# Layer-norm output transposed by DMA crossbar instead of TensorE, in a two-layer attention and MLP kernel

## Chip, cores and metric

The kernel runs on one core of one Trainium2 chip. The metric is the device time of one execution in microseconds (us); the kernel before has a median of 1329.79 us over three runs (1329.6 to 1330.23). Engines are named as in the profile: PE is TensorE, PEld its weight loads, DVE is VectorE, ACT is ScalarE, POOL is GpSimd, SP is SyncE, which here issues nearly all DMAs (its queue is written SPq).

## What is computed

Two layers over 2048 tokens of width 1024. Each layer is a layer norm, an attention over a dilated window (32 heads of 32, 8 positions two apart), a residual, a second layer norm, an MLP with a squared ReLU (3584 wide) and a second residual. The reference, cut:

```python
def _layernorm(x, axis=-1, eps=1e-5):
    m = jnp.mean(x, axis=axis, keepdims=True)
    v = jnp.var(x, axis=axis, keepdims=True)
    return (x - m) / jnp.sqrt(v + eps)
...
    x = x + _A_ref(_layernorm(x, axis=-1), A_wqkv, A_wo)
    x = x + _B_ref(_layernorm(x, axis=-1), B_w1, B_b1, B_w2, B_b2)
    x = x + _A_ref(_layernorm(x, axis=-1), A_wqkv, A_wo)
    x = x + _B_ref(_layernorm(x, axis=-1), B_w1, B_b1, B_w2, B_b2)
```

`_A_ref` is the projection to q, k and v, the window attention and the output projection; `_B_ref` is `w1`, squared ReLU, `w2`. All matrix operands are bf16.

## The kernel before

**Units.** The tokens are cut into four blocks of 512 (`BLK`), and each block in each layer is one unit `u`, so there are eight units, 0 to 3 in layer 0 and 4 to 7 in layer 1. A block has four tiles `tl` of 128 tokens. A unit goes through six stages, each a generator:

- **SA** (`gen_SA`): loads four x tiles (`xt`), normalises each and writes it transposed into `xnT`, a buffer of 128 partitions x 8 x 512, where TensorE needs the 1024 features on the partitions.
- **SQa**, **SQb** (`gen_SQ`): the projections; 64 matmuls each for k and q (SQa) and 64 for v (SQb), line 268, eight to one PSUM tile `pq`; ACT copies each out (line 270) into kT, qT or vT.
- **S2** (`gen_S2`): the window attention, nearly all on DVE (lines 316 to 414), with small matmuls (`lg`, line 362; in unit 0 line 349) and 16 TensorE transposes of its own for each half block (`ptp`, line 398).
- **SW** (`gen_SW`): the output projection, 64 matmuls (line 457), two groups of eight for each tile; DVE adds the residual into `xm` (line 459); then the second layer norm of that tile, into a second `xnT`.
- **SF** (`gen_SF`): the MLP in two halves; 28 groups of eight matmuls `ph` (line 485), each of which reads `xnT` of all four tiles, ACT's ReLU and square (lines 489, 490), and the second product (line 506) with the residual added by DVE (lines 512 to 521). Results go to `xs` in HBM (layer 0, line 522) or to the output (line 517).

**Order.** `build` lists the main stages: SQa(0), SQb(0), then for each u SQa(u+1), SW(u), SQb(u+1), SF(u). SA and S2 are side tasks, advanced in steps between those of the main stages, by a launch position and a deadline: SA(u) is launched 30 steps before SQa(u) and paced to be done after 0.75 of them. So SA's work lies within the MLP of another unit, while between SW(u), which ends in layer norms, and SF(u), which needs them, lies only SQb(u+1), and for the last unit nothing. The order of instructions on each engine is fixed when the program is built, from this order and from priorities (`high_priority`); each engine runs its own list in order and waits by semaphores.

**The layer norm** (`ln_transpose`, lines 160 to 198) works on one tile. In most units ACT does all: a sum (line 181), a sum of squares (line 185), small steps (lines 183, 187 to 189), and the scaled copy into `xn` (line 190). In SA(0) and SW(7) (`dve_stats`) DVE takes the statistics (line 172) and ACT only scales. `xn` has two buffers (`xp`, bufs=2, line 65), and lines 181 and 185 use it as scratch, so a tile's layer norm can start only when the tile two before it has been read. Then eight TensorE transposes against an identity (line 193) go into one PSUM tile `pt`, and one copy takes it to `xnT` (line 198 on DVE; line 196 on ACT in SA(1), SA(2) and SW(0), by `evac_act`). `pt` shares two PSUM buffers with `ptp`. `xnT` has two buffers (line 217), used in turn by SA and SW. There are 64 calls of `ln_transpose`: eight units, two norms, four tiles.

**Weights** come in tiles of up to 1 MB (`wt`, five buffers, lines 143 to 158). `get_w` issues loads up to three tiles ahead (`PF` = 3) of the one it hands out, so such a load waits until the tile five before it has been used. All loads and stores of x, xs, the weights and the output are issued by SP, in one queue.

Of the kernel before, what the change touches and what calls it, by code (L numbers as in the profile page):

```python
# [6 lines left out]
BF = mybir.dt.bfloat16  # L7
# [19 lines left out]
class _Kernel:  # L27
# [132 lines left out]
    def ln_transpose(self, xt, xnT, tl, dve_stats=False, evac_act=False):  # L160
        nc = self.nc
        small = self.small
        D = self.D
        xn = self.xp.tile([128, D], BF, name="xn", tag="xn")
        rstd = small.tile([128, 1], F32, name="rstd")
        nmr = small.tile([128, 1], F32, name="nmr")
        if dve_stats:
            nsg = D // 512
            stats = small.tile([128, nsg, nc.vector.BN_STATS_DIM], F32, name="stats")
            xr = xt.rearrange("p (n f) -> p n f", f=512)  # L170
            for sg in range(nsg):
                nc.vector.bn_stats(out=stats[:, sg, :], in_=xr[:, sg, :])
            mv = small.tile([128, nc.vector.BN_AGGR_DIM], F32, name="mv")
            nc.vector.bn_aggr(out=mv[:], in_=stats[:])
            lnv = small.tile([128, 1], F32, name="lnv")
            nc.scalar.activation(out=lnv[:], in_=mv[:, 1:2], func=ACTF.Ln, bias=self.eps[:], scale=1.0)
            nc.scalar.activation(out=rstd[:], in_=lnv[:], func=ACTF.Exp, scale=-0.5)
            nc.vector.scalar_tensor_tensor(out=nmr[:], in0=mv[:, 0:1], scalar=-1.0, in1=rstd[:], op0=ALU.mult, op1=ALU.mult)
        else:
            s1 = small.tile([128, 1], F32, name="s1")  # L180
            nc.scalar.activation(out=xn[:], in_=xt, func=ACTF.Identity, accum_out=s1[:])  # L181
            nmean = small.tile([128, 1], F32, name="nmean")
            nc.scalar.activation(out=nmean[:], in_=s1[:], func=ACTF.Identity, scale=-1.0 / D)
            s2 = small.tile([128, 1], F32, name="s2")
            nc.scalar.activation(out=xn[:], in_=xt, func=ACTF.Square, bias=nmean[:], scale=1.0, accum_out=s2[:])  # L185
            lnv = small.tile([128, 1], F32, name="lnv")
            nc.scalar.activation(out=lnv[:], in_=s2[:], func=ACTF.Ln, bias=self.eps[:], scale=1.0 / D)
            nc.scalar.activation(out=rstd[:], in_=lnv[:], func=ACTF.Exp, scale=-0.5)
            nc.scalar.activation(out=nmr[:], in_=nmean[:], func=ACTF.Identity, scale=rstd[:])
        nc.scalar.activation(out=xn[:], in_=xt, func=ACTF.Identity, bias=nmr[:], scale=rstd[:])  # L190
        pt = self.ps_t.tile([128, self.KD, 128], BF, name="pt", tag="pt")
        for kd in range(self.KD):
            nc.tensor.transpose(pt[:, kd, :], xn[:, kd * 128:(kd + 1) * 128], self.ident[:])  # L193
        with self.tc.high_priority():
            if evac_act:
                nc.scalar.copy(xnT[:, :, tl * 128:(tl + 1) * 128], pt[:])
            else:
                nc.vector.tensor_copy(xnT[:, :, tl * 128:(tl + 1) * 128], pt[:])  # L198

    def load_x_tile(self, layer, t, tag):  # L200
        nc = self.nc
# [458 lines left out]
```

## Time and profile before

| | |
|---|---|
| time, three runs | 1329.79 us median, 1329.6 to 1330.23 |
| profiled execution | span 1328.2 us from its first to its last instruction; its time outside the span is not recorded, and the median of the runs is 1.6 us longer |
| granted TensorE clock, mean | 0.996 |
| busy | PE 1284.9 us, PEld 679.9, DVE 830.1, ACT 681.1 |
| DMA | 223.69 MB, 168 GB/s on average |
| TensorE transposes of the layer norm (line 193) | 512, in 64 groups of eight |
| copies of the transposed tiles | 52 on DVE (685 ns each), 12 on ACT (1010 ns median) |

The units 1 to 5 repeat each other to within a few hundredths of a microsecond, 161 us apart: what is read in the stretch from 399 to 560 us holds for them. A stretch of 161 us has the last norms of one unit (SW) near its start and SA of the unit after the next near its end. The rows used below show, in order: the start in us, the duration, the engine, the line, the operation, output<-input, shape, how many instructions were merged, and in brackets the idle time of the engine before it with what ended it.

### The profile page before, as it was taken

The numbers are of one execution on the slowest core, as the hardware profiler recorded it, in microseconds if no ns is written. First come the engines' busy times: TensorE is split into PE (matmuls) and PEld (weight loads), VectorE is DVE, ScalarE is ACT, GpSimd is POOL, SyncE is SP. The second block draws the span as 40 slices with busy tenths as digits, with TensorE's granted clock in tenths as the row PEclk, the third lists the DMA queues.
The fourth block names the chain that finished last, engine by engine and source line by source line (L and its number), as shares of the span: only waits on it lengthen the run. The fifth ranks groups of instructions, "written<-read, shape, count | busy, mean of one in ns | idle before, by whom it ended". The sixth has DMA issues, their size and how long they took to land.

```text
span 1328.2 us, 17261 instructions
## 1 busy us (share of the span) xinstructions
PE 1284.9 (97%) x6972; PEld 679.9 (51%) x7104; DVE 830.1 (63%) x1170; ACT 681.1 (51%) x1229; POOL 2.9 (0%) x9
## 2 busy tenths in 40 slices
PE   6999999999999999999999999999999999997998
PEld 3665444654446544455445554455544555443443
DVE  4599993394934949268582777719676197926011
ACT  4647826287342964239561494615836166142622
POOL 0000000000000000000000000000000000000000
PEclk9999999999999999999999999999999999999999
DMA  8434544546355554656356464456634564346441
GB/s 214 160 127 158 175 142 156 194 160 204 123 196 186 180 174 143 205 184 208 121 178 230 161 220 152 135 188 208 204 127 163 195 214 138 123 150 224 127 135 56
DMA packets 180847, 223.69 MB, mean 168 GB/s; under 512 B 8608, under 2 KB 143776, under 8 KB 180768
## 3 DMA queue, kind: packets, MB, share of 16 engines
q1 hardware_dynamic: 177168, 222.58, 50.9%
q0 software_dynamic: 3600, 0.01, 0.4%
q8 instruction: 55, 0.90, 0.3%
q14 instruction: 24, 0.20, 0.0%
HBM read 209.98 MB, written 12.58 MB: 168 GB/s over the span
## 4 chain that ended last, share of the span: by engine, by line
PE 73%; DVE 14%; ACT 11%; issue 1%; DMA 0%; SPq 0%; ACTq 0%
PE ph L485 28%; PE pq L268 12%; DVE P L316 5%; DVE P L335 4%; ACT xn L190 3%; ACT xn L181 3%; ACT xn L185 2%; PE pt L193 1%; DVE pr L411 1%; PE py L457 1%; PE ptp L398 1%; DVE xm L459 1%; ACT vT L270 1%; PE lg L362 1%; DVE pr L412 1%
## 5 line engine op out<-in xcount | busy, mean ns | idle before, releaser
L485 PE MATMUL ph<-xnT,wt 128*128 128x512 bf16 x1751 | 393.1, 380 | 3.0 <-DVE xnT L198 0.8
L268 PE MATMUL pq<-xnT,wt 128*128 128x512 bf16 x1500 | 340.7, 381 | 3.0 <-DVE xnT L198 0.8
L506 PEld LDWEIGHTS <-r2t 128*128 128x128 bf16 x1792 | 174.6, 98 | 207.0 <-ACT r2t L490 0.4
L485 PEld LDWEIGHTS <-wt 128*128 128x128 bf16 x1792 | 174.2, 98 | 206.6 <-issue 2.9
L268 PEld LDWEIGHTS <-wt 128*128 128x128 bf16 x1536 | 216.7, 144 | 107.3 <-issue 3.3
L489 ACT ACTIVATE r<-ph,b1T 128x512 bf16<-128x512 f32 x224 | 153.0, 683 | 98.3 <-PE ph L485 96.9
L411 DVE TENSOR_TENSOR pr<-pb,vT 128x2048 bf16<-128x2048 bf16 x128 | 154.5, 1221 | 44.2 <-ACT pb L399 44.2
L316 DVE TENSOR_TENSOR P<-qT,kT 128x2048 bf16<-128x2048 bf16 x128 | 153.5, 1224 | 36.8 <-ACT qT L270 36.7
L490 ACT ACTIVATE r2t<-r 128x512 bf16<-128x512 bf16 x224 | 140.7, 629 | 5.5
L270 ACT CAST kT<-pq 128x512 bf16<-128x512 f32 x64 | 37.6, 587 | 189.1 <-PE pq L268 189.1
L457 PE MATMUL py<-wt,oT 128*128 128x512 bf16 x496 | 114.0, 383 | 0.8
L335 DVE TENSOR_TENSOR P<-P 128x2048 bf16<-128x2048 bf16 x84 | 102.2, 1218 | 0.4
L412 DVE TENSOR_TENSOR pr<-pr 128x1024 bf16<-128x1024 bf16 x128 | 85.6, 682 | 0.0
L399 ACT COPY pb<-ptp 128x1024 bf16<-128x1024 bf16 x32 | 31.6, 1013 | 104.1 <-PE ptp L398 103.9
L457 PEld LDWEIGHTS <-oT 128*128 128x128 bf16 x512 | 50.1, 99 | 59.0 <-issue 2.0
L270 ACT CAST qT<-pq 128x512 bf16<-128x512 f32 x64 | 37.5, 586 | 65.3 <-PE pq L268 65.3
L193 PE MATMUL pt<-ident,xn 128*128 128x128 bf16 x512 | 41.5, 227 | 29.5 <-ACT xn L190 28.7
L193 PEld LDWEIGHTS <-xn 128*128 128x128 bf16 x512 | 32.4, 101 | 51.4 <-ACT xn L190 45.5
L279 DVE COPY khalo<-kT 128x56 bf16<-128x56 bf16 x8 | 1.4, 179 | 85.1 <-ACT kT L270 85.1
L198 DVE COPY xnT<-pt 128x1024 bf16<-128x1024 bf16 x52 | 35.6, 685 | 29.6 <-PE pt L193 29.6
L181 ACT ACTIVATE xn<-xt 128x1024 bf16<-128x1024 f32 (+1 forms) x28 | 29.5, 1053 | 44.5 <-PE pt L193 44.5
L413 DVE TENSOR_TENSOR pr<-pr 128x512 bf16<-128x512 bf16 x128 | 51.5, 416 | 0.0
(468 smaller groups left out, 1109.2 us busy)
## 6 DMA issues: line engine op xcount, KB each, us to landing
wt<-in_B_w_dram SPq DMA_DIRECT2D x88, 1024.0 KB, 6.0
wt<-in_A_wqkv_dram SPq DMA_DIRECT2D x48, 1024.0 KB, 6.1
wt<-in_B_w_dram SPq DMA_DIRECT2D x32, 768.0 KB, 4.6
wt<-in_A_wo_dram SPq DMA_DIRECT2D x16, 1024.0 KB, 6.1
xt<-xs_106 SPq DMA_DIRECT2D x32, 512.0 KB, 4.1
xt<-in_A_x_dram SPq DMA_DIRECT2D x32, 256.0 KB, 3.8
xs_106<-xof SPq DMA_DIRECT2D x32, 256.0 KB, 2.9
out_dram<-xo SPq DMA_DIRECT2D x32, 128.0 KB, 2.0
```

Source lines behind the costliest of these rows:

```text
L193: nc.tensor.transpose(pt[:, kd, :], xn[:, kd * 128:(kd + 1) * 128], self.ident[:])
L268: nc.tensor.matmul(pq[:], fetch(nm)[kd // 4][:, kd % 4, c0:D:8], xnT[:, kd, :], start=(kd == 0), stop=(kd == KD - 1))
L270: nc.scalar.copy(dst[:, c0, off:off + BLK], pq[:])
L316: pi = nc.vector.tensor_tensor(P[:], qT[:, c, None, hb * HB:(hb + 1) * HB].to_broadcast([128, W, HB]), _win_ap(kT[:, c, :], HALO + hb * HB ...
L335: nc.vector.tensor_tensor(other[:], other[:], cur[:], ALU.add)
L411: nc.vector.tensor_tensor(pr[:], pb[:], vwin, ALU.mult)
L412: nc.vector.tensor_tensor(pr[:, 0:4, :], pr[:, 0:4, :], pr[:, 4:8, :], ALU.add)
L457: nc.tensor.matmul(py[:], oT[:, c, tl * 128:(tl + 1) * 128], wos[db][:, c, :], start=(c == 0), stop=(c == NCH - 1))
L485: nc.tensor.matmul(ph[:], wt[:, kd, cc * 128:(cc + 1) * 128], xnT[:, kd, :], start=(kd == 0), stop=(kd == KD - 1))
L489: nc.scalar.activation(out=r[:], in_=ph[:], func=ACTF.Relu, bias=self.b1T[:, f_idx:f_idx + 1], scale=1.0)
L490: nc.scalar.activation(out=r2t[:], in_=r[:], func=ACTF.Square)
L506: nc.tensor.matmul(py[:], r2[kf][:, tl * 128:(tl + 1) * 128], w2s[gi][:, j, :], start=(kf == 0), stop=(kf == KFH - 1))
```

## The change

The transposes by TensorE and the copy out of PSUM are replaced by one DMA for each tile, issued by SP, that reads `xn` (128 tokens x 1024) in SBUF and writes it transposed into the 128 columns of `xnT` that belong to the tile (128 partitions x 8 x 128). With it go the PSUM tile `pt` and the choice of engine for the copy. Everything else stays, the two buffers of `xn` included, which are now read by the DMA.

```diff
         nc.scalar.activation(out=xn[:], in_=xt, func=ACTF.Identity, bias=nmr[:], scale=rstd[:])
-        pt = self.ps_t.tile([128, self.KD, 128], BF, name="pt", tag="pt")
-        for kd in range(self.KD):
-            nc.tensor.transpose(pt[:, kd, :], xn[:, kd * 128:(kd + 1) * 128], self.ident[:])
-        with self.tc.high_priority():
-            if evac_act:
-                nc.scalar.copy(xnT[:, :, tl * 128:(tl + 1) * 128], pt[:])
-            else:
-                nc.vector.tensor_copy(xnT[:, :, tl * 128:(tl + 1) * 128], pt[:])
+        nc.sync.dma_start_transpose(xnT[:, :, tl * 128:(tl + 1) * 128], xn[:])
```

## Prediction

> **What bounds the kernel now.** The page comes first: the busy times, the transposes' group, the DMA queues and issues.
>
> ```profile
> PE 1284.9 (97%) x6972; PEld 679.9 (51%) x7104; DVE 830.1 (63%) x1170; ACT 681.1 (51%) x1229; POOL 2.9 (0%) x9
> ...
> q1 hardware_dynamic: 177168, 222.58, 50.9%
> q0 software_dynamic: 3600, 0.01, 0.4%
> ...
> L193 PE MATMUL pt<-ident,xn 128*128 128x128 bf16 x512 | 41.5, 227 | 29.5 <-ACT xn L190 28.7
> ...
> xt<-in_A_x_dram SPq DMA_DIRECT2D x32, 256.0 KB, 3.8
> xs_106<-xof SPq DMA_DIRECT2D x32, 256.0 KB, 2.9
> ```
>
> PE is busy nearly all the span, so work taken from PE is worth its full time where PE has no other wait. Line 193's 29.5 us idle is 10.1 us of the start and short waits. The timeline of PE shows them where a unit goes from SW to SF:
>
> ```profile
> 426.89 9.66 PE L457 MATMUL py<-wt,oT 128*128 128x512 bf16 x43
> 437.45 0.62 PE L193 MATMUL pt<-ident,xn 128*128 128x128 bf16 x8 [0.90 <-ACT xn L190]
> 437.91 4.48 PE L457 MATMUL py<-wt,oT 128*128 128x512 bf16 x19
> 442.23 0.59 PE L268 MATMUL pq<-xnT,wt 128*128 128x512 bf16 x2
> 443.07 0.62 PE L193 MATMUL pt<-ident,xn 128*128 128x128 bf16 x8 [0.25 <-ACT xn L190]
> 443.53 5.78 PE L268 MATMUL pq<-xnT,wt 128*128 128x512 bf16 x25
> 449.50 0.62 PE L193 MATMUL pt<-ident,xn 128*128 128x128 bf16 x8 [0.19 <-ACT xn L190]
> ...
> 453.05 0.62 PE L193 MATMUL pt<-ident,xn 128*128 128x128 bf16 x8
> ...
> 459.32 1.03 PE L485 MATMUL ph<-xnT,wt 128*128 128x512 bf16 x4
> ```
>
> The next instruction starts 0.45 us after a group of eight transposes does. The last tile is transposed at 453.05, and ph starts at 459.32: 6 us of v matmuls (SQb) cover the copy. ACT is why the tiles come late; its timeline shows tile 0's norm, without a gap, and the later tiles:
>
> ```profile
> 432.58 1.06 ACT L181 ACTIVATE xn<-xm 128x1024 bf16<-128x1024 f32 x1 [4.90 <-DVE xm L459]
> ...
> 436.16 1.24 ACT L190 ACTIVATE xn<-xm,nmr,rstd 128x1024 bf16<-128x1024 f32 x1
> 437.31 1.04 ACT L181 ACTIVATE xn<-xm 128x1024 bf16<-128x1024 f32 x1
> ...
> 440.75 1.04 ACT L181 ACTIVATE xn<-xm 128x1024 bf16<-128x1024 f32 x1
> ...
> 444.29 1.04 ACT L181 ACTIVATE xn<-xm 128x1024 bf16<-128x1024 f32 x1
> ```
>
> A norm takes 4.8 us of ACT alone. Tile 2 starts (440.75) once tile 0's xn has been read (437.9), tile 3 (444.29) after tile 1's (443.5): two xn buffers.
>
> **Removed.** 64 groups x 0.45 us = 28.8 us of PE, at most. The waits in this stretch add 0.90 + 0.25 + 0.19 = 1.3 us a unit. The weight loads of the transposes lie under matmuls: nothing. 52 x 0.685 = 36 us of DVE and 12 x 1.0 us of ACT go too; neither bounds PE in the middle, so I count them only where named.
>
> **Added: 64 DMAs of 256 KB.** None is in the trace, so I bound L, the time from the end of xn to an xnT that PE may read. Below: the 256 KB store of xs, 2.9 us. The 256 KB load of xt takes 3.8. A packet of q0 (4 B) costs 0.004 x 16 x 1328.2 us / 3600 = 24 ns of an engine, one of q1 (1256 B) 61 ns: 24 ns + 0.03 ns a byte. A store of 2 KB rows is 8 packets an engine, 0.7 us, so its fixed part is 2.2 us. In rows of 128 features (256 B) the transpose is 64 packets of 31 ns, 2.0 us: L = 4.2. If each 32-byte piece (16 tokens of a feature) costs a packet, it is 512 x 25 ns = 12.8 us: L = 15, the upper end. I take 4.2, nearest the two rows of equal size. At 2.0 us each, 64 transposes add 128 us to DMA engines busy for half of 1328 us: hidden.
>
> The trace has eight 128x128 transposes in 0.45 us. The Trainium skill, page "VectorE: DVE Perf Modes", section "The three transpose paths", lists 390 ns for one on TensorE and 1309 ns on the DMA crossbar. No run here has that second figure; taken eight times it would be an estimate of 10.5 us, and by it the sum would end near 1415, slower.
>
> **The stretch again.** Without groups and waits PE reaches ph at 459.32 - 1.8 - 1.3 = 456.2. On ACT tile 0 ends at 437.4 and lands at 441.6; tile 1 ends at 442.1 and lands at 446.3, or at 449 if it queues behind the two weight loads that SP issues from 440.70 (6 us each). Tile 2 runs from 442.1, tile 3 from 446.3 to 449, with v copies of 0.57 us between them: xn of tile 3 ends between 453.6 and 455, say 454.2, and lands at 458.4. So ph gains 0.9 us, and PE idles 2.2. What is late next is this landing.
>
> Idleness has a price: in unit 0, after a wait of 2.40 us, 21 matmuls take 6.38 us where 216 ns each would make 4.5; 1.8 us lost.
>
> ```profile
> 112.27 0.62 PE L193 MATMUL pt<-ident,xn 128*128 128x128 bf16 x8 [2.40 <-ACT xn L190]
> 112.72 6.38 PE L457 MATMUL py<-wt,oT 128*128 128x512 bf16 x21
> ```
>
> I take 2.4 us as the point where it starts. The Trainium skill, page "TensorE: Matmul & The Clock Gate", section "Why this matters for your kernels", puts that point at about 3 us. No wait between 1 and 2.4 us in this trace tells more, and the row speaks against the rule; at L = 4.2 the sum is the same by both, at 4.6 it would be 1322 by the rule and 1334 by the row.
>
> **The sum, against the span of 1328.2 us:**
> - units 1 to 6: 0.9 in SW, and 4 x 0.45 = 1.8 in SA, which lies inside SF where PE is full and the landing has some 17 us (from the last transposes, 382.2, to the first pq, 399.3, in the timeline): 2.7 x 6 = 16.2 gained;
> - SA(1): 4 x 0.45 = 1.8 gained;
> - unit 0's SW: PE could be at ph at 135.16 - 1.8 - 2.7 - 1.8 = 128.9; the last xn comes at about 128.5 (130.5 less two ACT copies), lands at 132.7, and a cold restart costs 1.8: 0.7 gained;
> - last unit: xn ends at 1224.3, 1.4 earlier without two copies and a group ahead of it, lands at 1227.2, ph was at 1226.3: 0.9 lost;
> - start: xn ends at 15.0. SP issues five weight loads from 3.1 to 11.2; with x and b2b that is 6.25 MB, of which 264 GB/s bring 4.5 by 17 us. Behind all of it the last tile lands near 23.5, free of it at 19.2. Middle 21.4 against 16.93: 4.5 lost.
>
> Gain 13.3 us: span 1314.9. The runs' median is 1.6 us above the span: **1317**.
>
> SP is also passed. A transpose waits there for its xn and for its xnT buffer, with weight loads, x loads and stores behind it. A w1 tile is loaded four tiles of 6.9 us ahead and lands in 6: some 20 us of cover. If that went, each further microsecond would be PE's.
>
> **Rivals.**
> 1. **All hidden.** L = 2.9, as the store. Tile 3 lands at 456.2, when PE comes: 3.1 + 1.8 = 4.9 a unit, x 6 = 29 gained, 4 in units 0 and 1, 2 lost at the ends: 1299. For it: the bytes are the same. Against: rows cut to 256 B.
> 2. **The landing takes the wait's place, and costs more.** Each microsecond of L delays tile 3 once by itself and about once more through the xn buffers: 2 x 6 + 2 at the ends = 14 us, and past 2.4 us idle the 1.8 us restart comes on top in six units, 11 us. It decides from L of about 4.4, where PE's idle time reaches 2.4: the gain is then 13 - 3 - 11, below zero. L = 6 gives 13 - 25 - 11 = -23: 1353. L = 7.5 gives 1374. For it: ACT's chain has no slack. Against: 256 KB land in 3.8 us now.
> 3. **The crossbar bounds.** 12.8 us x 64 = 819 us of DMA on 676 now: more than the span, about 1500. Were the change to move single 2-byte elements instead of using the crossbar, 8192 x 24 ns = 197 us each, it would be ten times the span. Nothing but the small-packet row speaks for these.
> 4. **SP's order.** Tile 3's transpose queued behind the weight load that waits for the end of the v matmuls (458.65): 3 to 6 us later in each unit, with the restart: about 1350. Against: loads are listed when their buffers come free, after xn.
>
> **Chances.** Forecast (L from 3.4 to 4.4, or later without the restart: 1306 to 1328) 0.36, of which 0.03 is within 0.2% (about what a measurement tells from no change); rival 1 0.16; rival 2 0.30, of which 0.03 is within; rival 3 0.10; rival 4 0.08. Faster 0.33 + 0.16 = 0.49, same 0.06, slower 0.45. The range leaves out rival 3 and the tails of 1 and 2: 1296 to 1375. The likeliest case's own range is 1306 to 1328.
>
> **What would show it.** PE without line 193; the transposes' time to landing (4.2 right, over 4.4 wrong); PE's idle before ph in SW's last stretch (2.2 us in each unit) with DMA as its releaser; ph's first matmuls at 216 ns, not 400; ACT line 181 waiting for a DMA; the first pq near 21. What makes it wrong most easily: L, or ACT blocked by the two xn buffers ahead of the v copies.

## The result and the profile after

The changed kernel takes 1333.73 us (median of 18 runs, 1328.84 to 1337.71), the kernel before 1330.59 (18 runs beside them, 1329.52 to 1331.63). The ratio is 1.0023, with a 95% interval of 1.0015 to 1.0032: slower by 0.2%, just clear of noise, where 1.0% faster was forecast. The profiled execution took 1334.27 us, with a span of 1332.6; its mean granted TensorE clock was 0.988, against 0.996 before.

Line numbers of the changed kernel are 7 lower than before, from the transpose (now line 191) on. The page after, then its list of DMA issues and its waits (engine and line, what it waited for, total us, times, longest):

```profile
PE 1264.9 (95%) x6592; PEld 654.0 (49%) x6592; DVE 799.1 (60%) x1118; ACT 667.4 (50%) x1217; POOL 2.9 (0%) x9
...
q1 hardware_dynamic: 244752, 239.37, 58.9%
```

```profile
xnT<-xn SPq DMA_TRANSPOSE x64, 3.4
```

```profile
PE pq L261 <- DMA xnT<-xn: 23.3, 1, 23.3
PE ph L478 <- DMA xnT<-xn: 14.0, 3, 11.0
PE py L499 <- ACT r2t L483: 9.2, 8, 2.7
...
ACT xn L181 <- DMA xnT<-xn: 6.2, 13, 1.2
...
ACT xn L190 <- DMA xnT<-xn: 5.2, 2, 4.6
```

PE lost 20 us of busy time, and yet the span grew. The transposes land in 3.4 us (median, from the issue on SP), so they are not slow. Besides the forecast waits ahead of ph, three kinds of waiting are new or longer: at the start (23.3 us until the first pq, against 16.9 before), at the last unit (11.0), and, of a kind that no rival named, waits of the second MLP product (py, line 499) for ACT's square `r2t`. The starts of the stages on PE's timeline tell where the time went. Gains are positive:

| stretch | before | after | gain, us |
|---|---|---|---|
| start to SW(0), its first py | 100.85 | 109.07 | -8.2 |
| SW(0) to ph(0) | 34.31 | 32.73 | +1.6 |
| ph(0) to SQa(2) | 102.99 | 102.52 | +0.5 |
| SQa(u+1) to ph(u), units 1 to 6, each | 59.99 to 60.08 | 59.86, 57.48, 57.86, 57.38, 58.80, 58.14 | +10.8 in all |
| ph(u) to SQa(u+2), units 1 to 5, each | 101.06 to 101.07 | 101.13, 103.01, 103.11, 102.61, 101.32 | -5.8 in all |
| ph(6) to SW(7) | 99.28 | 99.28 | 0 |
| SW(7) to ph(7) | 23.19 | 24.94 | -1.7 |
| ph(7) to the end | | | -1.5 |

The sum is -4.4, the difference of the spans. So the stretch with SW's transposes gains more than forecast, and the MLP, from which four groups of TensorE transposes (1.8 us) were taken, takes 1.5 to 2.0 us longer than before in units 2, 3 and 4. PE's timeline of unit 2 after, and its last row's counterpart in unit 3:

```profile
459.64 1.93 PE L261 MATMUL pq<-xnT,wt 128*128 128x512 bf16 x8
462.79 15.70 PE L478 MATMUL ph<-xnT,wt 128*128 128x512 bf16 x72 [1.23 <-ACT xn L185]
...
488.25 1.89 PE L478 MATMUL ph<-xnT,wt 128*128 128x512 bf16 x8 [0.33 <-ACT r L482]
...
495.94 0.39 PE L499 MATMUL py<-wt,r2t 128*128 128x512 bf16 x1 [0.16 <-ACT r2t L483]
499.07 14.20 PE L499 MATMUL py<-wt,r2t 128*128 128x512 bf16 x65 [2.75 <-ACT r2t L483]
...
658.36 15.88 PE L499 MATMUL py<-wt,r2t 128*128 128x512 bf16 x65 [1.98 <-ACT r2t L483]
```

The 1.23 us ahead of ph is put down to ACT, but that instruction has nothing to do with it: SP issues the last transpose at 459.53, and ph starts 3.3 us later, a landing's time. The 2.75 us wait is the new one. In unit 3 the wait is shorter, but the same 65 matmuls take 1.7 us longer: the granted clock was 0.5, half of full speed, from 658.4 to 661.8.

Such half-clock stretches are the second thing that the change added. After the start, the clock records show 0.5 for 10.2 us of the span before and for 30.7 us after, in pieces of 3.4 us or a whole multiple of it. Half of PE's busy time in them, an estimate of what they cost, is 3.7 us before and 10.9 after. In the MLP of units 0, 1 and 5 they follow a wait ahead of ph (2.42, 3.60 and 2.54 us) and cost 1.3 to 1.7 us each; the table counts that in the row of the MLP.

ACT's timeline shows why r2t is late; first before, with the row of PE that ends its wait, then after:

```profile
489.13 0.71 ACT L489 ACTIVATE r<-ph,b1T 128x512 bf16<-128x512 f32 x1
489.87 0.63 ACT L490 ACTIVATE r2t<-r 128x512 bf16<-128x512 bf16 x1
506.56 1.93 ACT L399 COPY pb<-ptp 128x1024 bf16<-128x1024 bf16 x2 [16.06 <-PE ptp L398]
517.38 1.06 ACT L181 ACTIVATE xn<-xt 128x1024 bf16<-128x1024 f32 x1 [8.89 <-PE pt L193]
```

```profile
516.73 0.61 PE L193 MATMUL pt<-ident,xn 128*128 128x128 bf16 x8
```

```profile
468.21 1.23 ACT L190 ACTIVATE xn<-xt,nmr,rstd 128x1024 bf16<-128x1024 f32 x1
...
472.51 1.23 ACT L190 ACTIVATE xn<-xt,nmr,rstd 128x1024 bf16<-128x1024 f32 x1
...
476.07 1.06 ACT L181 ACTIVATE xn<-xt 128x1024 bf16<-128x1024 f32 x1 [1.75 <-DMA xt<-xs]
...
486.39 1.24 ACT L190 ACTIVATE xn<-xt,nmr,rstd 128x1024 bf16<-128x1024 f32 x1
...
497.25 1.25 ACT L190 ACTIVATE xn<-xt,nmr,rstd 128x1024 bf16<-128x1024 f32 x1
498.38 0.64 ACT L483 ACTIVATE r2t<-r 128x512 bf16<-128x512 bf16 x1
```

Before, ACT normalises SA's first two tiles by 461.8, ahead of the MLP's ReLUs and squares, and finishes the squares of the first half at 490.5. The third tile's norm then waits 8.9 us until TensorE has transposed the first tile and freed its xn, 57 us after that was written. After, a DMA frees xn within a few microseconds, and SA's third and fourth norm and the last step of the first two (the rows `xn<-xt`) run between the ReLUs and squares of the first half. The last square ends at 499.0, when PE's py resumes. ACT's list itself differs: the order is fixed when the program is built, and without the transposes the third and fourth norms stand earlier in it.

The start: SP's timeline, then the ACT row that waits, then PE's first row.

```profile
3.14 1.07 SPq L149 DMA_DIRECT2D wt<-in_A_wqkv_dram  x2
10.22 4.97 SPq L191 DMA_TRANSPOSE xnT<-xn  x2
15.24 0.58 SPq L149 DMA_DIRECT2D wt<-in_A_wqkv_dram  x1
18.57 2.61 SPq L191 DMA_TRANSPOSE xnT<-xn  x2
21.23 1.14 SPq L149 DMA_DIRECT2D wt<-in_A_wqkv_dram  x2
```

```profile
17.30 2.37 ACT L190 ACTIVATE xn<-xt,nmr,rstd 128x1024 bf16<-128x1024 bf16 x2 [4.58 <-DMA xnT<-xn]
```

Before, SP issued five weight loads by 11.2 us. Now it stands at the first transpose from 4.2 to 10.2 with three of the loads behind it, and tile 2's norm waits 4.6 us for tile 0's transpose to have read its xn. A late weight load costs PE another 2.6 us at 60 us, and a half-clock stretch follows.

### The profile page after: what moved, and what is told of

Read it like the earlier page. It is cut to its first block, busy times and chain, and to the rows that moved or that the text cites. A ratio compares the mean times of both kernels' runs of the same rounds, so it can differ in the third digit from the quotient of the medians.

```text
span 1332.6 us, 16456 instructions
## 1 busy us (share of the span) xinstructions
PE 1264.9 (95%) x6592; PEld 654.0 (49%) x6592; DVE 799.1 (60%) x1118; ACT 667.4 (50%) x1217; POOL 2.9 (0%) x9
## 4 chain that ended last, share of the span: by engine, by line
PE 56%; ACT 22%; DVE 12%; DMA 8%; issue 2%; SPq 0%; ACTq 0%
PE py L499 28%; PE ph L478 18%; PE pq L261 9%; DMA xnT<-xn 5%; DVE P L309 4%; ACT r L482 4%; ACT xn L181 3%; ACT xn L185 3%; ACT r2t L483 3%; ACT xn L190 3%; DVE P L328 3%; DMA xt<-in_A_x_dram 1%; DVE pr L404 1%; DMA xt<-xs 1%; ACT vT L263 1%
## 5 line engine op out<-in xcount | busy, mean ns | idle before, releaser
L478 PE MATMUL ph<-xnT,wt 128*128 128x512 bf16 x1792 | 399.4, 384 | 25.7 <-DMA xnT<-xn 14.0
L499 PE MATMUL py<-wt,r2t 128*128 128x512 bf16 x1792 | 393.6, 380 | 9.2 <-ACT r2t L483 9.2
L261 PE MATMUL pq<-xnT,wt 128*128 128x512 bf16 x1536 | 341.9, 382 | 25.9 <-DMA xnT<-xn 23.3
L509 DVE TENSOR_TENSOR xo<-py,xm 128x512 bf16<-128x512 f32 x32 | 22.1, 692 | 113.2 <-PE py L499 113.2
L505 DVE TENSOR_TENSOR xm<-py,xm 128x512 f32<-128x512 f32 x64 | 43.9, 685 | 57.5 <-PE py L499 57.5
L514 DVE TENSOR_TENSOR xof<-py,xm 128x512 f32<-128x512 f32 x32 | 22.1, 692 | 91.5 <-PE py L499 76.6
```

The costliest lines, as they stand in the source:

```text
L261: nc.tensor.matmul(pq[:], fetch(nm)[kd // 4][:, kd % 4, c0:D:8], xnT[:, kd, :], start=(kd == 0), stop=(kd == KD - 1))
L478: nc.tensor.matmul(ph[:], wt[:, kd, cc * 128:(cc + 1) * 128], xnT[:, kd, :], start=(kd == 0), stop=(kd == KD - 1))
L499: nc.tensor.matmul(py[:], r2[kf][:, tl * 128:(tl + 1) * 128], w2s[gi][:, j, :], start=(kf == 0), stop=(kf == KFH - 1))
```

## The experiments

**Theory A**: the two ends lose what the landings cost there. **Theory B**: in the middle, TensorE's transposes, at their place in PE's order, held SA's norms back by way of the two xn buffers. DMAs free SA's buffers early, so the norms are placed and run early, where ACT is busiest, and the MLP waits for ACT. **Rival C**: the middle is limited by the landing of tile 3 before ph and by the two xn buffers.

All times below are medians of 4 to 11 runs beside runs of the kernel before on the same chip (1330.2 to 1330.6). Stage times and rows are of one profiled execution each, which lies up to 5 us from its median.

**TensorE at the ends.** SA(0) and SW(7) keep the eight transposes and the copy.

```diff
+        if dma:
             nc.sync.dma_start_transpose(xnT[:, :, tl * 128:(tl + 1) * 128], xn[:])
+            return
+        pt = self.ps_t.tile([128, self.KD, 128], BF, name="pt", tag="pt")
...
-            self.ln_transpose(xt, xnT, tl, ...)
+            self.ln_transpose(xt, xnT, tl, ..., dma=(u > 0))
-            self.ln_transpose(xm[:], xnT, tl, ...)
+            self.ln_transpose(xm[:], xnT, tl, ..., dma=(u < self.n_layers * self.NB - 1))
```

> TensorE transposes are kept in SA(0) and SW(7), the two places with no other work beside them; the other 56 stay DMAs. In the trace of after, the first pq starts 6.4 us later than before, py of unit 0 8.2 later, ph of unit 0 6.6 later, and ph of the last unit loses 1.8 us more and then 1.5 us to a cold restart. Theory A (the loss is at the two ends and the middle gains a little): 1333.7 - 6.6 - 3.3 = about 1324, first pq at 17 us, ph of unit 7 less than 5 us after its py ends. Rival (the ends are swallowed later, because DVE or ACT sets the pace of unit 0): less than 4 us gained, above 1329.

Measured: 1322.26 us, ratio 0.9939 (0.9922 to 0.9957); first pq at 16.7, SW(7) to ph(7) 23.2 as before. The ends cost 11 us, a little more than A had counted. The MLP's stretches stay long (102.4, 104.0, 103.1, 102.9 and 101.2 us, half-clock stretches included); the profiled execution, 1327.2 us, was the slowest of six that spread over 9.1 us.

**SA's norms held on ACT.** All 64 stay DMAs; one ordering edge puts each SA norm behind the last square recorded before it.

```diff
-            nc.scalar.activation(out=xn[:], in_=xt, func=ACTF.Identity, accum_out=s1[:])
+            si = nc.scalar.activation(out=xn[:], in_=xt, func=ACTF.Identity, accum_out=s1[:])
+            if after is not None:
+                self.tc.add_manual_dep(si.ins, after.name, ...NoSync..., reason="hold the norm on ACT")
...
-            self.ln_transpose(xt, xnT, tl, ...)
+            self.ln_transpose(xt, xnT, tl, ..., after=self.last_r2)
...
-                        nc.scalar.activation(out=r2t[:], in_=r[:], func=ACTF.Square)
+                        self.last_r2 = nc.scalar.activation(out=r2t[:], in_=r[:], func=ACTF.Square).ins
```

> All 64 transposes stay DMAs; the first sum of each SA norm is put behind the last squared-ReLU instruction recorded before it on ACT (an order on one engine, no semaphore), so SA's norms can't run early in the MLP. Theory B (in the middle the gain is given back in SF, since without the TensorE transposes SA's norms run early, among ACT's ReLU and square of the first half, and py waits for r2t): the stretch from ph to the next SQa falls from 101.1 to 103.1 us in units 1 to 5 to about 99.3 each, 12 to 15 us in all, time 1319 to 1322, py's waits for r2t (9.2 us) near 0. Rival C (the middle is limited by the landing of tile 3 before ph): SF changes little, time within 3 us of 1333.7.

Measured: 1319.97 us, ratio 0.9913 (0.9900 to 0.9926), as B expected and far from C. The MLP stretch is 101.7, 100.2, 100.2, 100.2 and 101.9 us in units 1 to 5. Of the 12.2 us between the two spans, 7.0 are there and 2.4 from SW(0) to ph(0); the MLP alone gave less than the 12 to 15 that B had put on it. PE's waits for r2t fall from 9.2 to 4.4 us. Units 1 and 5 are longer by a half-clock stretch behind a wait ahead of ph (2.58 and 2.44 us); in all, these stretches cost 4.0 us less than in the changed kernel's profile (6.9 against 10.9, the same estimate), which is part of the 12.2 and which the hold was not made to change. PE's timeline of unit 3, second half of the MLP:

```profile
675.87 20.88 PE L483 MATMUL ph<-xnT,wt 128*128 128x512 bf16 x96
696.59 2.54 PE L504 MATMUL py<-wt,r2t 128*128 128x512 bf16 x11
699.86 18.52 PE L504 MATMUL py<-wt,r2t 128*128 128x512 bf16 x85 [0.73 <-ACT r2t L488]
718.22 1.03 PE L266 MATMUL pq<-xnT,wt 128*128 128x512 bf16 x4
```

The first half has no wait for r2t left; one of 0.73 us is new in the second half, where the norms now are. It is most of the difference between the 100.2 of a unit and the 99.3 expected.

**DMAs in SW alone** (28; `dma=False` in SA, and in SW as in the first experiment).

> DMA transposes only in SW(0) to SW(6), 28 of 64; SA and SW(7) keep TensorE. Theory B: SA's transposes at their place in TensorE's order hold SA's norms back as before, so SF keeps its 101.1 us, and the stretch from SQa to ph keeps what the DMAs gained (60.05 before, 57.4 to 58.8 in units 2 to 5 of after): 1 to 2.6 us in each of six units, time 1315 to 1325. Rival C: SW is where the landing hurts, so 1328 to 1335.

Measured: 1319.41 us, ratio 0.9919 (0.9906 to 0.9932). SQa to ph takes 57.5 to 58.3 us in units 2 to 6, and the MLP 101.06 to 101.07 in units 2 to 5: TensorE's transposes of SA hold its norms back again (the third norm of unit 3 waits 8.9 us for them, as before the change), and no wait for r2t is left. Rival C as a reason for the loss falls: SW is where the DMAs gain.

**DMAs in SA alone** (28; `dma=False` in SW, no hold).

> The mirror of the kernel with DMAs in SW alone: DMAs only in SA(1) to SA(7), not held; SA(0) and all SW keep TensorE. Theory B (SA's norms, no longer held by TensorE's order, run early and delay r2t): the stretch from ph to the next SQa is 101 to 103.5 us, no gain although 1.8 us of TensorE work left it, SQa to ph stays at 60.05 or grows: 1326 to 1335. If the crowding needs SW's DMAs as well, SF falls to 99.3 us: about 1318.

Measured: 1331.90 us, ratio 1.0006 (0.9997 to 1.0015). 12.6 us of TensorE work (28 groups of 0.45) went, for nothing. SQa to ph is 60.0 as before, the MLP 99.9 to 102.2, and PE waits 8.8 us for r2t. B holds without SW's DMAs too.

Two rows of unit 0 in this run bear on the prediction's price of idleness. They are at the place where before 21 matmuls took 6.38 us after a wait of 2.40:

```profile
110.94 0.62 PE L196 MATMUL pt<-ident,xn 128*128 128x128 bf16 x8 [2.38 <-ACT xn L190]
111.40 4.70 PE L460 MATMUL py<-wt,oT 128*128 128x512 bf16 x21
```

**Four xn buffers** in the changed kernel (`tag="xn", bufs=4`).

> The changed kernel with four xn buffers in place of two. Rival C (landing times two xn buffers limits the middle and the start): ACT waits at the xn writes (11.4 us of waits for xnT DMAs in all) vanish, ph comes about 2 us earlier in six units and the first pq 4 us earlier: about 1318. Theory B (SA's norms run early because nothing holds them): the start gains up to 4 us, but with more buffers SA's norms can run ahead still more, so SF loses as much or more than now: 1330 to 1337.

Measured: 1326.56 us, ratio 0.9969 (0.9957 to 0.9981): between the two expectations. The first pq comes at 20.4 and SW(0) at 103.2, so of the 8.2 us lost by SW(0) the two buffers made 5.9. The other 2.3 need not be the landing: with TensorE at the start, the hold and four buffers (below) the first pq comes at 16.8, and SW(0) still at 102.1, against 100.85 before. The MLP takes 100.6 to 101.6 in units 1 to 5, where B had expected as much as in the changed kernel or more, but SQa to ph is 58.4 to 58.6 in units 2 to 5. The crowd has moved: two of SA's norms now run on ACT around the last one of SW. PE's timeline of unit 3:

```profile
619.18 15.70 PE L478 MATMUL ph<-xnT,wt 128*128 128x512 bf16 x72 [2.13 <-ACT nmean L183]
```

ACT starts the last xn of SW 53.9 us after SQa (614.67 against 560.80), and the first of SA's at 618.22, ahead of ph. With the hold as well (below) SW's last xn starts 51.2 us after SQa.

**Control: the hold in the kernel before** (TensorE transposes throughout).

> Control: the kernel before (all TensorE transposes) with the hold on SA's norms alone. Theory B: TensorE's order held SA's third and fourth norms already, so the hold has little to give: SF stays at 101.1 us, and only the two norms that run early in SW's stretch move away, at most 1 us a unit: 1323 to 1330. If the hold helps for another reason than the change, it gives as much here as in the changed kernel: 1317 or less.

Measured: 1339.50 us, ratio 1.0066 (1.0054 to 1.0079): slower. The MLP grows from 101.07 to 102.59 us a unit. The hold gains nothing by itself; B expected a small gain and was wrong there. TensorE's transposes now wait in PE's order for the later norms:

```profile
699.15 0.62 PE L198 MATMUL pt<-ident,xn 128*128 128x128 bf16 x8 [0.40 <-ACT xn L195]
...
707.41 2.76 PE L511 MATMUL py<-wt,r2t 128*128 128x512 bf16 x12 [0.30 <-ACT r2t L495]
...
713.29 0.62 PE L198 MATMUL pt<-ident,xn 128*128 128x128 bf16 x8 [0.30 <-ACT xn L195]
```

These make 1.0 of the 1.5 us. So the order of ACT that suits the DMAs does not suit the transposes on PE, and the reverse.

**Ends and hold together** (56 DMAs).

> Both earlier edits together: TensorE transposes in SA(0) and SW(7), DMAs in the other 56, and SA's norms held on ACT behind the last squared-ReLU instruction. If the two losses (ends, and SA's norms running early) are separate, their gains add: the ends gave 11.5 us (1333.7 to 1322.3), the hold 13.8 (1333.7 to 1320.0), so about 1308 to 1311. If they are one (ACT's backlog starting from the late start), about 1318.

Measured: 1310.03 us, ratio 0.9846 (0.9830 to 0.9861): the two gains add (23.7 us together, 25.3 by the sum).

**And four xn buffers with them.**

> The kernel with both earlier edits and four xn buffers in place of two. If the xn buffers and the landing together still cost time before ph (Rival C as a part), ACT's waits for xnT DMAs vanish and ph comes earlier: 3 to 8 us below the two edits alone, 1303 to 1306. If ACT's own work is what makes tile 3 late, the time stays within 2 us of the two edits alone.

Measured: 1299.16 us, ratio 0.9763 (0.9750 to 0.9776): 2.4% faster than before, the best version, and 10.9 us below the two edits alone, more than C as a part had counted. SQa to ph takes 56.1 to 56.5 us. PE's timeline of unit 3:

```profile
604.82 15.70 PE L493 MATMUL ph<-xnT,wt 128*128 128x512 bf16 x71 [0.21 <-DMA xnT<-xn]
...
686.66 18.52 PE L514 MATMUL py<-wt,r2t 128*128 128x512 bf16 x84 [0.74 <-ACT r2t L498]
705.02 1.24 PE L276 MATMUL pq<-xnT,wt 128*128 128x512 bf16 x5
```

The timeline shows no other wait in the unit: beside these 0.95 us, PE's own work is all that is left, and the units 1 to 6 have no half-clock stretch. C is right as a part, once B's crowd is gone.

**All 64 by DMA, held, four xn buffers.**

> All 64 transposes by DMA, SA held, four xn buffers: against the kernel with TensorE at the ends it prices the ends once the xn buffers are gone as a cause. Landing alone: first pq at 20.4 us (3.5 later than before), the last ph 1.8 later with a restart of 1.5: 1299 + 7 = about 1306. If the ends still cost the 11 us that they cost with two buffers: about 1310.

Measured: 1303.61 us, ratio 0.9797 (0.9783 to 0.9810), first pq at 20.0. With four buffers the ends cost 4.5 us, where with two they cost 9.9 between the held kernels and 11.5 without the hold: the rest was the buffers.

**A second transpose behind each** in the kernel with ends and hold: 56 more DMAs of a constant tile into a scratch tile (two buffers) that nothing reads. A first form of it, on the kernel with four xn buffers and with a second transpose of xn itself, has no time: with the scratch tiles the program does not fit in SBUF (a pool that needs 12.6 KB a partition finds 9.1).

```diff
+            ti = nc.sync.dma_start_transpose(xnT[:, :, tl * 128:(tl + 1) * 128], xn[:])
+            xd = self.xp.tile([128, self.KD, 128], BF, name="xd", tag="xd")
+            di = nc.sync.dma_start_transpose(xd[:], self.b2b[:])
+            self.tc.add_manual_dep(di.ins, ti.ins.name, ...NoSync..., reason="behind the real one")
```

> The kernel with TensorE at the ends and SA held (two xn buffers, 1310.0 us), in which each of the 56 DMA transposes is followed by a second one of a constant tile into a scratch tile that nothing reads (the output is the reference's). It prices the DMAs themselves: 56 more transposes on SP's queue and on the DMA engines. If SP and the DMA engines have room (a transpose costs what waits for its landing, and nothing else), at most 3 us more. If SP's order or the DMA engines cost (rivals 3 and 4 of the prediction in a milder form), 10 us and more, with PE waits for weights or xnT.

Measured: 1335.78 us, ratio 1.0036 (1.0023 to 1.0048): 25.8 us more than without them. The expectation of at most 3 us fell. PE's timeline of unit 3, first without and then with the second transposes:

```profile
605.75 15.70 PE L493 MATMUL ph<-xnT,wt 128*128 128x512 bf16 x71 [1.44 <-DMA xnT<-xn]
```

```profile
623.66 17.14 PE L498 MATMUL ph<-xnT,wt 128*128 128x512 bf16 x71 [3.23 <-issue]
```

From the issue of tile 3's transpose to ph it is 3.4 us without (602.36 to 605.75) and 4.4 with (619.23 to 623.66); the means over the six units are the same. The 71 matmuls behind the longer wait run in part at half clock and take 1.4 us longer. By stages, SQa to ph costs 15.2 us more in six units, the MLP 10.8 in seven; after each of its seven waits ahead of ph, 2.3 to 4.4 us, a half-clock stretch follows; without the second transposes one did. PE waits for no weights. The size is near rival 2's price, 14 us for a microsecond of landing and 11 for the restarts, and so is the form: of the 15.2, 6.1 are the way from issue to ph and 8.3 a later end of tile 3's xn. But 3.6 of these 8.3 are something else, waits of pq for DVE's `xof`, which in turn waits up to 7.3 us for stores on SP's queue (3.9 without). Whether the second transpose delays the first on the DMA engines, or the next one on SP (each holds SP's queue 1.3 us or more), was not separated.

## Why the prediction was wrong

- **SA, the step that failed**: "4 x 0.45 = 1.8 in SA, which lies inside SF where PE is full". The MLP was to gain 10.8 us in units 0 to 5; it lost 5.4, 16.2 short, the largest part of the 17.7 us between forecast and span. Waits for r2t are 9.2 of it, and a half-clock stretch behind one of them 1.7; 4.5 are half-clock stretches behind the waits ahead of ph in units 0, 1 and 5, which are the landing's and not SA's (the one of unit 0 was forecast, with unit 0's SW, which gained 1.6 us without it where 0.7 with it was forecast). The transposes were work on PE, but also, through the two xn buffers, the brake that kept SA's third and fourth norms off ACT until PE reached them (the 8.89 us wait of line 181, which stood in the profile of before). I had counted ACT's order as given. The hold took the waits for r2t to 4.4 and gave 7.0 us back in the MLP of five units, DMAs in SA alone gained nothing, and with DMAs in SW alone no such wait is left: that is shown, not only argued. That the buffers are why the build placed the norms earlier is argued from the wait alone.
- **The landing** (4.2 us forecast): 3.4 from issue, 3.0 at the least and 10.3 at the most. The working held: 1056 packets a transpose were added (67,584 on q1, over 64), and, by the difference of the queue's shares, 27 us of engine time each, 1.7 on each of 16 engines, against 2.0. The estimate of 10.5 us falls with it: the 1309 ns that the Trainium skill, page "VectorE: DVE Perf Modes", section "The three transpose paths", lists for a 128x128 block on the DMA crossbar is not paid eight times by eight blocks in one DMA. No run here measures one block alone.
- **SW** (0.9 us a unit): the step was right and its landing too long. Tile 3's xn was to end 54.9 us after SQa starts (454.2 against 399.3), and it ended 54.1 to 56.6 us after it, 54.9 in the mean. The gain was 1.8 a unit (10.8 over six), since the landing was 0.9 shorter, with 1.1 to 3.6 us of idle PE ahead of ph, around the 2.2 forecast.
- **The start** (4.5 lost, and 1.8 gained in SA(1)): 8.2 lost by SW(0), 6.4 of them at the first pq (23.3, against 21.4 forecast). I had kept SP's order of before, with five weight loads ahead of the transposes; SP's new list has two, then waits, and ACT waits for xn. Four buffers brought 5.9 back.
- **The end** (0.9 lost): 3.2. 1.7 was landing. The rest was the clock: PE had been idle 11 us in one piece, where before transposes came in between, and its next matmuls lost 1.4 us more at half clock than before.
- **The restart**: 2.4 us is not a point where it starts. The row that the prediction read it from was in part chance: with DMAs in SA alone the same place has a wait of 2.38 us, and the same 21 matmuls take 4.70 us and not 6.38 (rows above). In the changed kernel waits of 1.98, 2.42, 2.54, 2.58 and 3.60 us were followed by half clock, waits of 1.88 and 2.12 and two of 2.75 were not. Over all the traces here, no wait up to 1.9 us was followed by it, every one from 2.8 on was, and between 1.96 and 2.75 both happened. The bound of about 3 us in the Trainium skill's "TensorE: Matmul & The Clock Gate", section "Why this matters for your kernels", does not hold in these rows: shorter waits were followed by half clock, too. So what a run with waits of 2 to 3 us loses is in part luck: of the 18 runs of the changed kernel the six fastest had a mean clock of 0.990 to 0.994, the six slowest 0.986 to 0.990. The 0.2% is the median over such runs, and the 7 us more that half clock cost in the profiled one are more than its whole loss of 4.4.
- **Rivals**: rival 1's condition was not met by the change; that its 1299 us is where the kernel ends with the three other edits is a coincidence. Rival 2's price was about met by the second transposes; its restarts took 4.5 us in the changed kernel, and it was not the main cause of the loss. Rival 3 did not happen. Rival 4 happened at the start only, in another form: loads behind transposes, not the reverse. The two xn buffers, which the prediction named as one thing that could make it wrong, did cost (5.9 us at the start, 10.9 with the two other edits), by another way than the one that failed.

What stays open: the 0.7 us wait for r2t that the held kernels keep; the last 1 to 2 us by which SW(0) comes late with four xn buffers; what decides whether a wait of 2 to 3 us is followed by half clock; and which of SP and the DMA engines made the second transposes cost.

## What to carry to other kernels

An operation that leaves the busiest engine may also have been the brake on another engine's early work, through the buffers that it freed late: look in the profile of before for the waits that the removed instruction ended (here ACT's first sum, 8.9 us), and ask what runs earlier without it, and beside what. Where TensorE had read a tile at once, as in SW (0.45 us), a DMA holds its source longer (3.4 us), so its buffer count belongs to the change: with four xn buffers, SA's norms held and TensorE kept where nothing covers the landing, the same idea gave 2.4% in place of a loss of 0.2%.

## What the runs showed of the hardware

- A crossbar transpose of 128 x 1024 bf16, SBUF to SBUF, occupied SP's queue for 1.24 us at the least, against 0.37 (median) for a plain copy, and landed in 3.0 us at the least.
- The changed kernel's 18 runs spread over 8.9 us (1328.8 to 1337.7), those of the kernel before over 2.1, and the time went with the mean granted clock (0.994 to 0.986); four runs with DMAs in SW alone spread over 1.2, four with the ends, the hold and four buffers over 2.8.
- The granted clock fell to 0.5 in pieces of 3.4 us or a whole multiple, and one piece cost PE 1.3 to 1.7 us. It followed every idle wait of 2.8 us or more after the start, none of 1.9 or less, and some of those between (1.98 us was followed, 2.75 was not).
